# A Fourier filter and maxout MLP on one core: how batch 0 loads x, splits the weights and thresholds its spectrum

## The chip, the cores and the metric

The kernel runs on one core of a Trainium2 chip. The metric is the device time of one execution in microseconds (us). TensorE (PE in the profile), VectorE (DVE), ScalarE (ACT) and GpSimd (POOL) each run their own instruction queue in order; SyncE (SP) and ScalarE issue the DMAs.

## The reference, cut to what matters

```
X  = rfft(x, axis=1)                         # x: 8 batches, 3072 x 256, f32
Yr = X.real @ w_r - X.imag @ w_i + b_r
Yi = X.real @ w_i + X.imag @ w_r + b_i
Y  = sign(Y) * max(|Y| - 0.01, 0)            # on Yr and Yi apart: the soft threshold
y  = irfft(Y)                                # 24576 tokens x 256
h  = max(y @ w1, y @ w2, y @ w3)             # w1..w3: 256 x 768, float64
out = h @ w_out                              # w_out: 768 x 256, float64
```

The four MLP weights are given in float64.

## The kernel before, in words

The transform of 3072 points is split as 48 x 64. For each batch there are five stages. **Stage a** (`load_x`, `stage_a`) loads x in eight quarters q, transforms over the 48 and stores the result in DRAM (`a_d`). **Stage b** (`load_a`, `first_b` for batch 0) loads pairs of rows of it, k = 0 to 11, and transforms over the 64. **Stage w** (`first_w`, `soft_threshold`, `finish_w`) multiplies by w_r and w_i, adds the bias, thresholds at 0.01 and takes a maximum. **Stage q** (`first_q`) transforms back over the 64 and stores `z_d`. Then comes, chunk by chunk, the last transform (`load_z`, `split_z`, `inverse`) and the MLP (`up`, `down`).

Batches 1 to 7 go through this in f16 pairs (high and low halves), three products each, interleaved with the MLP of the batch ahead. Batch 0 has nothing to hide behind. It runs in f32 at the very start, and its code stands in `with in_order()`, where each engine's queue follows the order of the code; after that block the scheduler orders the queues.

The same start also prepares the weights. The float64 words of w1, w2, w3 and w_out come as pairs of 32-bit words; class `Weights` turns each of 18 units (12 of `w_up`, 6 of `w_dn`) into a scaled f16 pair. Its pieces are DVE work with a little ACT work: `exponent`, `combine`, `words`, for eight units `differ` (w1 - w3, w2 - w3), and `low`. Four units (w3) are instead transposed on TensorE in `turn`, which adds the two words' products up there. Each piece has a cost in a list, and `fill(budget)` in step k of batch 0 takes pieces off the list until the budget is spent; `fill` thus decides how much weight work a step carries. In step k the order on the queues is: stage b of k+1, the filling, stage w of k, stage q of k-1. So TensorE's product for stage q of k-1 (tile `pz`, line 580) needs the thresholded tile `uf` of k-1, and stands behind the products of stage w of k (tile `py`, lines 568 and 569).

At the start, the loads of batch 0's x go out on SP (r = 0) and ACT (r = 1), in rows of 2 KB, 96 of them a load; the f32 results leave in tiles `aq` and `zq`. `warm(36)` then runs 36 dummy products on a tile of zeros, and `load_fft_weights` loads w_r and w_i (`wst`), the bias, of which one row (partition 64) is written twice, and `qf`; after it `load_first_blocks(0)` loads the first table of stage b (`mb_all`). In `soft_threshold` DVE clips u to plus and minus 0.01 (`t`, line 633) and subtracts (line 634).

The lines of the weight work: 317 (`xe`), 320 (`xg`, ACT), 324 and 327 (`combine`), 334 and 335 (`words`), 341 (`differ`, two instructions), 347 (`turn`, TensorE), 351 and 357 (high halves, ACT), 354 (`turned`), 360 and 361 (`low`).

## Time and profile before

| | |
|---|---|
| median of 3 runs | 1837.19 us (1836.24 to 1837.34) |
| the profiled execution | 1839.4 us, span of its core 1837.6 us |
| TensorE busy in the span | 1788.9 us (97%) |
| VectorE busy | 1306.5 us (71%) |
| ScalarE busy | 961.7 us (52%) |
| granted TensorE clock, mean | 0.99 |

The profile is of one execution; times in it are microseconds from the span's start. Busy time of TensorE counts products that stream, so it tells where the engine stood still, not how well it was used. A row of the timeline has the start, the duration, the engine, the line, the operation and the tiles, and in brackets the idle time ahead of it with what ended that; for a queue of DMA issues (SPq, ACTq) the duration is that of issuing, not of the transfer.

### The profile page before, as it was taken

The numbers are of one execution on the slowest core, as the hardware profiler recorded it, in microseconds if no ns is written. First come the engines' busy times: TensorE is split into PE (matmuls) and PEld (weight loads), VectorE is DVE, ScalarE is ACT, GpSimd is POOL, SyncE is SP. The second block draws the span as 40 slices with busy tenths as digits, with TensorE's granted clock in tenths as the row PEclk, the third lists the DMA queues.
The fourth block names the chain that finished last, engine by engine and source line by source line (L and its number), as shares of the span: only waits on it lengthen the run. The fifth ranks groups of instructions, "written<-read, shape, count | busy, mean of one in ns | idle before, by whom it ended". The sixth has DMA issues, their size and how long they took to land.

```text
span 1837.6 us, 36331 instructions
## 1 busy us (share of the span) xinstructions
PE 1788.9 (97%) x14583; PEld 1287.7 (70%) x14583; DVE 1306.5 (71%) x2589; ACT 961.7 (52%) x1923; POOL 72.4 (4%) x120
## 2 busy tenths in 40 slices
PE   6988999999999999999999999999999999999999
PEld 2854777777677777767777776777767777777776
DVE  1898789667786688757886688866878568864443
ACT  1344666455555555455564565645655456544443
POOL 0001000000000000100001000000000000000000
PEclk8988999999999999999999999999999999999999
DMA  8734432233223323232322432223322312212110
GB/s 241 259 98 104 130 101 84 73 107 104 82 66 102 95 84 90 68 110 86 87 81 68 123 87 87 76 77 105 96 87 67 96 54 62 61 38 58 36 35 27
DMA packets 116443, 164.99 MB, mean 90 GB/s; under 512 B 13009, under 2 KB 88786, under 8 KB 116178
## 3 DMA queue, kind: packets, MB, share of 16 engines
q1 hardware_dynamic: 53122, 86.37, 17.1%
q10 hardware_dynamic: 63152, 76.31, 13.7%
q8 instruction: 114, 1.87, 0.4%
q14 instruction: 55, 0.45, 0.1%
HBM read 87.13 MB, written 75.50 MB: 88 GB/s over the span
## 4 chain that ended last, share of the span: by engine, by line
PE 72%; DVE 7%; issue 2%; DMA 1%; ACT 1%; ACTq 1%; SPq 0%; POOL 0%; DVEq 0%; POOLq 0%
PE pu L133 11%; PE pu L135 11%; PE pu L134 11%; PE pd L135 8%; PE pd L133 7%; PE pd L134 7%; PE py L134 2%; PE py L133 2%; PE py L135 2%; PE pa L485 2%; DMA xq<-in_x_dram 1%; DVE u L676 1%; PE pi L135 1%; DVE hh L128 1%; PE pi L133 1%
## 5 line engine op out<-in xcount | busy, mean ns | idle before, releaser
L133 PE MATMUL pu<-yh,w_all 128*128 128x384 f16 x1536 | 501.5, 327 | 5.3 <-DVE h L819 4.0
L134 PE MATMUL pu<-yl,w_all 128*128 128x384 f16 x1536 | 500.9, 326 | 2.4 <-DVE yl L128 2.1
L135 PE MATMUL pu<-yh,w_all 128*128 128x384 f16 x1536 | 500.3, 326 | 0.0
L127 ACT ACTIVATE hh<-h 128x384 f16<-128x384 f32 x384 | 200.4, 522 | 361.1 <-DVE h L819 354.1
L819 DVE TENSOR_TENSOR h<-pu,c 128x384 f32<-128x384 f32 x384 | 212.3, 553 | 174.9 <-PE pu L135 114.0
L135 PE MATMUL pd<-w_all,hh 128*128 128x256 f16 x1152 | 314.0, 273 | 8.4 <-DVE hh L128 8.2
L134 PE MATMUL pd<-w_all,hh 128*128 128x256 f16 x1152 | 314.2, 273 | 0.2 <-DVE w_all L361 0.2
L133 PE MATMUL pd<-w_all,hh 128*128 128x256 f16 x1152 | 313.9, 273 | 0.0
L128 DVE SCALAR_TENSOR_TENSOR hh<-h,hh 128x384 f16<-128x384 f32 x384 | 213.1, 555 | 105.5 <-ACT hh L127 104.2
L817 ACT ACTIVATE c<-pu 128x384 f32<-128x384 f32 x384 | 186.9, 487 | 132.3 <-PE pu L135 121.7
L133 PEld LDWEIGHTS <-w_all 128*128 128x128 f16 x1548 | 151.5, 98 | 113.5 <-issue 33.3
L135 PEld LDWEIGHTS <-w_all 128*128 128x128 f16 x1548 | 151.4, 98 | 104.6 <-issue 4.8
L134 PEld LDWEIGHTS <-w_all 128*128 128x128 f16 x1548 | 151.6, 98 | 87.4 <-issue 7.7
L676 DVE SCALAR_TENSOR_TENSOR u<-py,s1x,cs 64x256 f32<-64x256 f32 x308 | 148.7, 483 | 45.7 <-ACT cs L687 32.0
L133 PE MATMUL py<-wc_all,tt 128*128 128x256 f16 x504 | 137.4, 273 | 0.0
L134 PE MATMUL py<-wc_all,tt 128*128 128x256 f16 x504 | 137.4, 273 | 0.0
L135 PE MATMUL py<-wc_all,tt 128*128 128x256 f16 x504 | 137.4, 273 | 0.0
L133 PEld LDWEIGHTS <-hh 128*128 128x128 f16 x1152 | 112.8, 98 | 32.5 <-issue 2.4
L134 PEld LDWEIGHTS <-hh 128*128 128x128 f16 x1152 | 112.8, 98 | 30.9 <-issue 0.8
L135 PEld LDWEIGHTS <-hh 128*128 128x128 f16 x1152 | 112.8, 98 | 27.9 <-DVE hh L128 14.2
L846 ACT ACTIVATE o<-pd,s1u 128x256 f32<-128x256 f32 x192 | 83.5, 468 | 70.9 <-PE pu L135 26.1
L472 DVE TENSOR_REDUCE mxx<-xq 112x1 f32<-112x512 f32 x112 | 74.5, 678 | 46.6 <-DMA xq<-in_x_dram 42.2
(196 smaller groups left out, 3058.8 us busy)
## 6 DMA issues: line engine op xcount, KB each, us to landing
z_d<-zs ACTq DMA_DIRECT2D x96, 256.0 KB, 2.2
zq<-z_d SPq DMA_DIRECT2D x128, 192.0 KB, 3.1
out_dram<-o ACTq DMA_DIRECT2D x192, 128.0 KB, 2.3
a_d<-aq ACTq DMA_DIRECT2D x118, 192.0 KB, 3.2
aj<-a_d SPq DMA_DIRECT2D x86, 256.0 KB, 3.1
xq<-in_x_dram SPq DMA_DIRECT2D x114, 192.0 KB, 3.6
rw<-in_moe_w_dram SPq DMA_DIRECT2D x12, 384.0 KB, 6.3
mb_all<-in_dft_ib_dram SPq DMA_DIRECT2D x4, 384.0 KB, 5.4
```

The costliest lines, as they stand in the source:

```text
L127: nc.scalar.activation(out=hi, in_=src, func=AF.Copy, scale=scale)
L128: nc.vector.scalar_tensor_tensor(out=lo, in0=src, scalar=scale, in1=h, op0=ALU.mult, op1=ALU.subtract)
L133: nc.tensor.matmul(o, lh, rh, start=start, stop=False, **kw)
L134: nc.tensor.matmul(o, lh, rl, start=False, stop=False, **kw)
L135: nc.tensor.matmul(o, ll, rh, start=False, stop=stop, **kw)
L472: nc.vector.tensor_reduce(out=batch(b, "x")[0:XR, 2 * q4 + i:2 * q4 + i + 1], in_=xp, axis=AX.X, op=ALU.max, apply_absolute_value=True,)
L485: nc.tensor.matmul(pa[r][64 * c:64 * c + 64], fr[rows], xs[c][rows], start=True, stop=True)
L676: nc.vector.scalar_tensor_tensor(out=u[64 * c:64 * c + 64, j], in0=pk[r], scalar=inv[r], in1=c1[r], op0=ALU.mult, op1=ALU.add,)
L817: nc.scalar.activation(out=c1, in_=pu[0], func=AF.Relu)
L819: nc.vector.tensor_tensor(out=h32, in0=pu[1], in1=c1, op=ALU.max)
L846: nc.scalar.activation(out=o, in_=pd[t], func=AF.Copy, scale=st[b, "su"][1])
```

## The change

It has five parts, all in batch 0 and in the weight work. (1) x of batch 0 is loaded in four groups g, in rows of 8 KB (four tiles' worth of a partition at once), all on SP; `first_a` does stage a for a group with the same 32 products and 16 copies and stores each group with two DMAs in place of four. The tile `aq` is twice as wide with 2 buffers in place of 3 plus `zq`. (2) The five bias loads write each row once, and `load_first_blocks(0)` goes ahead of the loads of w_r and w_i. (3) `words` makes one f32 of a 64-bit word's two halves, so that `differ`, `low` and `turn` handle one word in place of two. (4) The threshold of steps 0 to 10 is two Relu activations on ACT and one subtraction on DVE. (5) The budgets change: the maxima of `w_dn` move from steps 7 and 8 to 5 and 6, step 10 has 1.5, step 11 carries no filling, and the filling behind the last stage q has 3.0 in place of 4.0. The zeros of `warm` are taken from `wsh`, which is written later.

```diff
 def load_fft_weights():
+        load_first_blocks(0)
...
-        for j in range(2):
-            for c in range(2):
-                nc.sync.dma_start(
-                    out=bias[64 * c:64 * c + 64, j, :], in_=rows[c].broadcast_to([64, D])
-                )
-        nc.sync.dma_start(out=bias[64:65, 1, :], in_=rows[0])
+        for c, j, r0, r1 in ((0, 0, 0, 64), (0, 1, 0, 64), (1, 0, 64, 128), (1, 1, 65, 128), (0, 1, 64, 65)):
+            nc.sync.dma_start(out=bias[r0:r1, j, :], in_=rows[c].broadcast_to([r1 - r0, D]))
...
             def words():
-                nc.vector.tensor_tensor(out=hw, in0=hw, in1=g, op=ALU.bitwise_or)
                 nc.vector.scalar_tensor_tensor(
-                    out=r, in0=lw, scalar=2.0**-52, in1=g.bitcast(F32), op0=ALU.mult, op1=ALU.mult
+                    out=r, in0=lw, scalar=2.0**-32, in1=hw, op0=ALU.mult, op1=ALU.add
                 )
+                nc.vector.scalar_tensor_tensor(
+                    out=m, in0=r, scalar=2.0**20, in1=t["g"].bitcast(F32), op0=ALU.add, op1=ALU.mult
+                )
             def differ():
-                for v, bv in zip((m, r), (self.raw[base][:, :, 1], self.raw[base][:, :, 0])):
-                    nc.vector.tensor_tensor(out=v, in0=v, in1=bv.bitcast(F32), op=ALU.subtract)
+                nc.vector.tensor_tensor(
+                    out=m, in0=m, in1=self.raw[base][:, :, 1].bitcast(F32), op=ALU.subtract
+                )
...
             def low():
-                nc.vector.tensor_tensor(out=m, in0=m, in1=hi, op=ALU.subtract)
-                nc.vector.tensor_tensor(out=lo, in0=m, in1=r, op=ALU.add)
+                nc.vector.tensor_tensor(out=lo, in0=m, in1=hi, op=ALU.subtract)
...
+    def first_x(g):
+        xv = x[0].rearrange("(n1 r g w n) d -> g w r n1 (n d)", n1=N1, r=2, g=4, w=2)[g]
...
+            for r in range(2):
+                nc.sync.dma_start(
+                    out=xw[64 * r:64 * r + N1, 2048 * g:2048 * g + 2048].rearrange("p (w m) -> p w m", w=2),
+                    in_=xv[:, r].rearrange("w p m -> p w m"),
+                )
...
+    def first_a(g):
+        aq = quad_tile("aq")
...
+        for c in range(2):
+            (nc.scalar if c else nc.sync).dma_start(
+                out=av[c], in_=aq[64 * c:64 * c + N1].rearrange("p (r m) -> p r m", r=2)
+            )
...
     def soft_threshold(k, u):
         t = fft.tile([P, 2, D], F32, name="t", bufs=1)
+        if k < NJP - 1:
+            nc.scalar.activation(out=t, in_=u, func=AF.Relu, scale=-1.0, bias=nlam)
+            nc.scalar.activation(out=u, in_=u, func=AF.Relu, scale=1.0, bias=nlam)
+            nc.vector.tensor_tensor(out=u, in0=u, in1=t, op=ALU.subtract)
...
-            elif 4 <= k < NJP:
-                fill(2.8)
+            elif 4 <= k < NJP - 2:
+                fill(3.0)
+            elif k == NJP - 2:
+                fill(1.5)
```

In the queues this stands as follows. First SP, from the loads of w_r and w_i on (`wst`; `mb_all` is the first table of stage b). Before:

```order
L185 DMA wst<-in_w_i_dram 128x256
L189 DMA bias<-in_b_r_dram 64x256
L189 DMA bias<-in_b_i_dram 64x256
...
L192 DMA bias<-in_b_r_dram 1x256
L193 DMA qf<-in_dft_ib_dram 128x256
L854 DMA mb_all<-in_dft_ib_dram 128x768
L284 DMA rw<-in_moe_w_dram 128x768 x8
```

and in the change, from batch 0's x on:

```order
L468 DMA w_all<-in_x_dram 48x2048 x6
L477 DMA xq<-in_x_dram 48x1024 x4
L923 DMA id_sb<-in_ident_dram 128x128
L498 DMA a_d<-aq 96x1x1024 x4
L891 DMA mb_all<-in_dft_ib_dram 128x768
L188 DMA wst<-in_w_r_dram 128x256
L188 DMA wst<-in_w_i_dram 128x256
...
L191 DMA bias<-in_b_r_dram 64x256 x2
L191 DMA bias<-in_b_i_dram 64x256
L191 DMA bias<-in_b_i_dram 63x256
L191 DMA bias<-in_b_r_dram 1x256
L192 DMA qf<-in_dft_ib_dram 128x256
```

The table now stands ahead of the weights and of the bias; the one-row bias load writes a row that no other load writes.

Second DVE, in steps 0 and 1 of batch 0 (`uf` is the tile that is thresholded, `mwu` the maxima of the weights). Before:

```order
L572 TENSOR_TENSOR uf<-py,bias 128x512
L633 TENSOR_SCALAR t<-uf 128x512
L634 TENSOR_TENSOR uf<-uf,t 128x512
L712 TENSOR_REDUCE mxu<-uf 128x1
L288 TENSOR_REDUCE mwu<-rw 128x1 x5
```

and in the change, where the subtraction follows the addition at once:

```order
L603 TENSOR_TENSOR uf<-py,bias 128x512
L667 TENSOR_TENSOR uf<-uf,t 128x512
L749 TENSOR_REDUCE mxu<-uf 128x1
L287 TENSOR_REDUCE mwu<-rw 128x1 x5
L603 TENSOR_TENSOR uf<-py,bias 128x512
```

while ACT has, in one of those steps:

```order
L577 ACTIVATE tf<-px 128x4x128
L580 ACTIVATE tf<-px 128x4x64
L665 ACTIVATE t<-uf,nlam 128x512
L666 ACTIVATE uf<-uf,nlam 128x512
L768 ACTIVATE zs<-pz 128x512
L769 DMA z_d<-zs 128x2x256
```

The two activations stand between DVE's addition and DVE's subtraction, and nothing was moved into the gap on DVE.

From the f16 split of batch 1's first pair (`ah` on ACT, `al` on DVE) to the end, the queues of all engines are the same row for row.

## Rows read from the trace of the kernel before

**Rows 1.** Busy time by stage, in six stretches from the span's start: busy us of each engine (in brackets the instructions), then the granted TensorE clock as a share of full speed, the DMA engines' mean busy share, and GB/s.

```profile
0.00:39.64 39.64, 21.56 (x101) 7.08 (x101) 8.67 (x14) 6.48 (x10) 2.61 (x7) 0.89 0.86 222
39.64:47.53 7.89, 7.89 (x34) 7.28 (x35) 0.00 (x0) 1.74 (x4) 0.00 (x0) 0.68 1.00 370
47.53:116.63 69.10, 62.91 (x316) 51.19 (x319) 63.40 (x141) 24.18 (x48) 0.57 (x3) 0.97 0.60 189
116.63:175.40 58.77, 51.97 (x309) 26.27 (x309) 57.59 (x151) 30.48 (x63) 5.65 (x6) 0.86 0.41 106
175.40:198.95 23.55, 23.36 (x182) 14.27 (x179) 11.39 (x34) 12.07 (x24) 3.77 (x4) 1.00 0.57 164
198.95:1837.60 1638.65, 1621.20 (x13654) 1181.63 (x13651) 1165.42 (x2250) 886.78 (x1776) 59.77 (x100) 1.00 0.28 79
```

**Rows 2.** Timeline of TensorE at the start: start us, duration us, engine, line, operation, tiles, count, and in brackets the idle time ahead and its releaser.

```profile
20.21 7.93 PE L859 MATMUL pw<-zero 128*128 128x512 f16 x36 [0.32 <-ACT aq L488]
39.64 3.75 PE L541 MATMUL px<-mb_all,ga_all 128*128 128x128 f32 x16 [11.50 <-DMA mb_all<-in_dft_ib_dram]
...
47.37 1.05 PE L541 MATMUL px<-mb_all,ga_all 128*128 128x128 f32 x8
...
52.57 1.05 PE L541 MATMUL px<-mb_all,ga_all 128*128 128x128 f32 x8
```

**Rows 3.** Timeline of SP's queue of DMA issues: start us, duration us of the issue, queue, line, tiles.

```profile
30.42 0.47 SPq L189 DMA_DIRECT2D bias<-in_b_i_dram  x1
35.52 0.29 SPq L192 DMA_DIRECT2D bias<-in_b_r_dram  x1
...
36.25 0.42 SPq L854 DMA_DIRECT2D mb_all<-in_dft_ib_dram  x1
```

**Rows 4.** Timeline of ACT's queue of DMA issues: the last store of batch 0's stage a, and the first loads of stage b, which wait for all the stores.

```profile
24.54 0.36 ACTq L492 DMA_DIRECT2D a_d<-zq  x1
28.87 1.45 ACTq L517 DMA_DIRECT2D ga_all<-a_d  x3
```

**Rows 5.** The loads of stage b into tile `ga_all`, from 0 to 60 us: time from issue to landing, shortest, median and longest.

```profile
DMA to landing us min/median/max: 4.5/6.2/8.5
```

**Rows 6.** Busy time by stretch, with the columns of rows 1: while batch 0's x lands in rows of 2 KB (2 to 18), while stores in rows of 4 KB make up most (18 to 22), while MLP weights land in rows of 3 KB (40 to 50), and while two loads of batch 1's x, in the same rows of 2 KB, go beside other loads (66 to 70).

```profile
2.00:18.00 16.00, 12.10 (x56) 3.17 (x56) 2.76 (x4) 3.67 (x5) 0.00 (x0) 1.00 1.06 212
18.00:22.00 4.00, 3.32 (x21) 1.29 (x18) 1.96 (x3) 1.26 (x3) 1.89 (x2) 1.00 1.03 386
40.00:50.00 10.00, 10.00 (x49) 9.19 (x49) 2.33 (x4) 2.62 (x6) 0.00 (x0) 0.77 1.01 374
66.00:70.00 4.00, 4.00 (x22) 3.24 (x22) 3.48 (x10) 2.10 (x4) 0.00 (x0) 1.00 1.13 389
```

**Rows 7.** Timeline of DVE in batch 0: one threshold and the first maximum of the weights behind it, the addition of step 3, then a `differ` and a `low` with what follows each.

```profile
47.57 0.69 DVE L572 TENSOR_TENSOR uf<-py,bias 128x512 f32<-128x512 f32 x1 [8.67 <-PE py L569]
48.29 0.43 DVE L633 TENSOR_SCALAR t<-uf 128x512 f32<-128x512 f32 x1
48.75 0.69 DVE L634 TENSOR_TENSOR uf<-uf,t 128x512 f32<-128x512 f32 x1
49.48 0.69 DVE L712 TENSOR_REDUCE mxu<-uf 128x1 f32<-128x512 f32 x1
50.08 0.54 DVE L288 TENSOR_REDUCE mwu<-rw 128x1 f32<-128x384 f32 x1
...
62.32 0.69 DVE L572 TENSOR_TENSOR uf<-py,bias 128x512 f32<-128x512 f32 x1 [1.43 <-PE py L569]
...
78.38 1.02 DVE L341 TENSOR_TENSOR rw<-rw 128x384 f32<-128x384 f32 x2
79.32 0.35 DVE L317 TENSOR_SCALAR xe<-rw 128x384 uint32<-128x384 uint32 x1
...
86.40 0.55 DVE L360 TENSOR_TENSOR rw<-rw,w_all 128x384 f32<-128x384 f32 x1
86.99 0.56 DVE L361 TENSOR_TENSOR w_all<-rw 128x384 f16<-128x384 f32 x1
87.46 0.68 DVE L572 TENSOR_TENSOR uf<-py,bias 128x512 f32<-128x512 f32 x1
```

**Rows 8.** Timeline of ACT: two activations back to back on tiles of 512 and 256 columns in PSUM, and one on 512 columns in SBUF that also reads a one-column tile.

```profile
64.45 0.60 ACT L546 ACTIVATE tf<-px 128x512 f32<-128x512 f32 x1 [0.44 <-PE px L541]
64.94 0.38 ACT L549 ACTIVATE tf<-px 128x256 f32<-128x256 f32 x1
...
198.21 0.71 ACT L127 ACTIVATE ah<-aj,s0x 128x512 f16<-128x512 f32 x1
```

**Rows 9.** Waits of TensorE from 47.53 to 116.63 us: for whom, us in total, times, longest.

```profile
PE pz L583 <- DVE uf L634: 5.3, 1, 5.3
PE pz L580 <- DVE uf L634: 0.8, 1, 0.8
```

**Rows 10.** Groups of DVE instructions by line and shape from 47 to 199 us (busy us in all, mean ns of one): `low`'s first instruction for w_out.

```profile
L360 DVE TENSOR_TENSOR rd<-rd,w_all 128x256 f32<-128x256 f32 x6 | 2.5, 411 | 0.0
```

**Rows 11.** TensorE alone in stretches of 2 us: busy us and instructions, granted clock, DMA share, GB/s.

```profile
30.00:32.00 2.00, 0.00 (x0) 0.75 0.53 175
...
160.00:162.00 2.00, 1.13 (x11) 1.00 0.00 0
162.00:164.00 2.00, 0.99 (x22) 1.00 0.97 220
164.00:166.00 2.00, 2.00 (x7) 0.53 1.03 253
```

More of the change, by code (lines that the diff above doesn't have):

```diff
@@ L345, in turn @@
                 for j in range(width // P):
-                    for v, first in ((m, True), (r, False)):
-                        nc.tensor.matmul(
-                            pt[:, j * P:j * P + P], v[:, j * P:j * P + P], id_sb, start=first, stop=not first
-                        )
+                    nc.tensor.matmul(
+                        pt[:, j * P:j * P + P], m[:, j * P:j * P + P], id_sb, start=True, stop=True
+                    )
                 t["p"] = pv = pt[:, 0:width].rearrange("p (f d) -> p f d", d=P)
@@ L466, in load_x @@
         st["x", q] = [xq[0:XR, c] for c in range(2)]
+    def first_x(g):
+        xv = x[0].rearrange("(n1 r g w n) d -> g w r n1 (n d)", n1=N1, r=2, g=4, w=2)[g]
+        xw = w_all.bitcast(F32)
+        if g < 3:
+            st["x0", g] = [xw[:, 2048 * g + 512 * i:2048 * g + 512 * i + 512] for i in range(4)]
+            for r in range(2):
[3 more added lines that the diff above has]
+                )
+            return
+        st["x0", g] = []
+        for w in range(2):
+            xq = fft.tile([P, 2, 2 * D], F32, name="xq", bufs=2)
+            for r in range(2):
+                nc.sync.dma_start(out=xq[64 * r:64 * r + N1].rearrange("p c m -> p (c m)"), in_=xv[w, r])
+            st["x0", g] += [xq[:, 0], xq[:, 1]]
@@ new lines, in first_a @@
+    def first_a(g):
+        aq = quad_tile("aq")
+        for i in range(2):
+            pa = [ff_tile("pa") for _ in range(2)]
+            for c in range(2):
+                for r in range(2):
+                    rows = slice(64 * r, 64 * r + N1)
+                    nc.tensor.matmul(
+                        pa[r][64 * c:64 * c + 64], fr[rows], st["x0", g][2 * c + i][rows], start=True, stop=True
+                    )
+            for r in range(2):
+                o = aq[:, 1024 * r + 512 * i:1024 * r + 512 * i + 512]
+                if r == 0:
+                    nc.scalar.activation(out=o, in_=pa[r][0:XR], func=AF.Copy)
+                else:
+                    nc.vector.tensor_copy(out=o, in_=pa[r][0:XR])
+        av = batch(0, "a").rearrange("k (r g c n) d -> g c k r (n d)", r=2, g=4, c=2)[g]
+        for c in range(2):
+            (nc.scalar if c else nc.sync).dma_start(
+                out=av[c], in_=aq[64 * c:64 * c + N1].rearrange("p (r m) -> p r m", r=2)
+            )
@@ L478, in stage_a @@
         b, q4 = divmod(q, NCH)
-        aq = quad_tile("zq") if q < NCH and q % 4 == 3 else quad_tile("aq")
+        aq = quad_tile("aq")[:, 0:NQ * D]
         xs = st["x", q]
@@ L486, in stage_a @@
         for r in range(2):
[L487 to L490 removed]
+            nc.scalar.activation(out=aq[:, r * 512:r * 512 + 512], in_=pa[r][0:XR], func=AF.Copy)
         for c in range(2):
[L492 removed]
+            nc.scalar.dma_start(
                 out=batch(b, "a")[:, 8 * q4 + 4 * c:8 * q4 + 4 * c + 4, :],
@@ L879, in fourier_maxout_kernel @@
         nc.sync.dma_start(out=fr, in_=fa)
+        nc.gpsimd.memset(nlam, -LAM)
         nc.gpsimd.memset(zero, 0.0)
-        for q in range(NCH):
-            load_x(q)
+        for g in range(4):
+            first_x(g)
         nc.sync.dma_start(out=id_sb, in_=ident)
-        for q in range(NCH):
-            stage_a(q)
+        for g in range(4):
+            first_a(g)
         warm(36)
@@ L952, in fourier_maxout_kernel @@
         warm(12)
-        fill(4.0)
+        fill(3.0)
         split_z(0, 2)
```

45 lines of the change are left out of this document (19 added, 26 removed).

## The prediction

> **What bounds the kernel now.** Read first the busy time by stage [rows 1]. After 198.95 us TensorE is busy 1621.20 of 1638.65 us at full clock, and from there the change leaves every queue as it was; I take that stretch as unchanged. All that can move lies in the first 198.95 us, in three places.
>
> Until 39.64 us TensorE waits for data: 21.56 us busy, of which 7.93 are the dummy products of `warm` [rows 1, 2]. What ended that wait is in the timelines. Stage b's first product starts at 39.64 us, released by the table `mb_all` [rows 2]. That table was issued at 36.25 us, because SP stood from 30.42 to 35.52 us at the one-row bias load, which has to wait for the load that wrote the same row [rows 3]. The other input was there sooner: ACT issued the loads of `ga_all` at 28.87 us, and the quickest took 4.5 us, so about 33.4 us [rows 4, 5]. Behind that stands batch 0's x: its 3072 x 256 f32 are 3.15 MB, and they moved at 212 GB/s with the DMA engines full (1.06), where other transfers reach 374 to 389 GB/s [rows 6].
>
> From 47.53 us, the end of the first `py`, to 116.63 us, where the maximum over all of batch 0 is taken, a step of TensorE is 5.20 us (47.37 to 52.57) [rows 2], but DVE is busy 63.40 of 69.10 us [rows 1]. Its last waits for TensorE are 8.67 us ahead of step 0 and 1.43 us ahead of step 3 [rows 7]; from then on DVE sets the pace, and TensorE loses 5.3 + 0.8 us to it at the end [rows 9].
>
> From 116.63 to 175.40 us DVE is busy 57.59 of 58.77 us, TensorE 51.97 with its clock at 0.86 [rows 1]: DVE-bound again. Then TensorE is full until 198.95 us.
>
> **The change part by part.**
>
> *Start.* Removing the double write takes SP's wait away, and `mb_all` now stands ahead of the weights and biases, so the table no longer sets the start; `ga_all` does. That alone moves stage b from 39.64 to 33.4 us: -6.3. What is late next is the chain x, stage a, stores, `ga_all`. How fast rows of 8 KB land when they are the only traffic, no row shows. Bounds: 212 GB/s as now, and 389 GB/s [rows 6]. I take 340: nearer to the upper end, since batch 1's x in rows of 2 KB is part of the 389, so neither its spacing nor its 48 partitions cap it alone. 3.15 MB take 14.9 us at 212 and 9.3 at 340: -5.6 (0 to -6.8). One queue instead of two costs nothing I can see: the 374 GB/s are mostly one queue's (SP). The ring of `aq` still holds the same amount of unsaved results (two double tiles for four single ones), so the store of one group still delays the copy of the next but one, as before. Stage b then starts near 27.8 us. Its first products run cold, as now: the clock had fallen by 30 to 32 us [rows 11], some 3 us after `warm` ended at 28.14 [rows 2], and the new chain leaves a gap of about that size too. If the gap closes, up to 2.4 us more are won: the first 16 products take 3.75 us for twice 0.89 warm. **Start: -11.9 us, from -6.3 to -15.**
>
> *Threshold.* On DVE one step now takes 0.72 (addition) + 0.46 (clip) + 0.73 (subtraction) + 0.60 (maximum) = 2.51 us, from 47.57 to 50.08 [rows 7]. In the change the clip goes, but the subtraction stands right behind the addition in DVE's queue and must wait for two activations. A 512-column activation from SBUF with a one-column operand takes 0.71 us, and the second starts some 0.11 us before the first ends [rows 8]: 0.60 + 0.71 = 1.31. With 0.1 for the two handovers (an estimate from the 0.03 between dependent DVE instructions there, 48.26 to 48.29) the step takes 0.72 + 1.41 + 0.73 + 0.60 = 3.46: +0.95 us. What is queued behind the waiting subtraction is the weight work, and TensorE's `pz` waits for the subtraction. Bounds: +0.6 (activations at the 0.60 of a PSUM source) and +1.7 (another activation of 0.7 ahead in ACT's queue). Steps 0 to 2 have the 1.43 us of slack ahead of step 3: 2.85 - 1.43 = +1.4. Steps 3 to 10 have none: 8 x 0.95 = +7.6. Both are on the path.
>
> *Weight work in batch 0's steps.* Up to the last step the queue does the same units as before. `differ` drops one of two instructions: two take 0.94 (78.38 to 79.32), so -0.47. `low` drops one of two: 1.06 for both (86.40 to 87.46), 0.47 for one, so -0.59 [rows 7]. Four units each: -4.2. `words` keeps two instructions, but the second now reads the first's result; a dependent instruction starts 0.03 after its forerunner ends and an independent one 0.08 before (48.29 against 50.08 [rows 7]), so +0.1 for six units, +0.6. The sum of this and the threshold is 1.4 + 7.6 - 4.2 + 0.6 = **+5.4 us for 47.53 to 116.63** (bounds 0 and +11). The new budgets move work within the steps; step 11 has none, but steps 4 to 10 carry what it had, so that is neutral while DVE is full. The two transposes lose half their products; TensorE has slack there: nothing.
>
> *Weight work behind it.* Four more `differ` (-1.9), four `low` (-1.9, at 0.47, since the interleaved order hides the handover) and six `low` of w_out at 0.41 less 0.08 of overlap (-2.0) [rows 7, 10]: -5.8. The smaller filling ahead of the first chunk leaves 1.0 us more for later. **-4.8 us**, bounds 0 (TensorE or batch 1's x sets the end) and -8 (the falls of the clock in this stretch vanish too).
>
> **Sum:** -11.9 + 5.4 - 4.8 = -11.3. The profiled execution is 1839.4 us, so 1828.1 there; it lies 2.2 above the median of the runs, 1837.19, against which I state the time: **1825.9 us**.
>
> [...] Rows of the trace: x at 212 GB/s, 2 KB rows, 64 KB from one partition's row to the next [rows 6]. [...]
>
> **Rivals.**
>
> [...] Then the start gains 6.3 and the sum is -6.3 + 5.4 - 4.8 = -5.7: 1831.5 us. Chance 0.25.
>
> *B, the round trip to ACT is hidden.* If DVE's wait costs as much as the clip it replaces, 47.53 to 116.63 us gains 4.2 - 0.6 and the sum is -11.9 - 3.6 - 4.8 = -20: 1817 us. For: ACT is busy 24.18 of 69.10 us [rows 1], so it is free when asked. Against: DVE's order, with nothing between addition and subtraction. Chance 0.10.
>
> *C, slower: TensorE's clock falls in the steps.* With DVE at 6.5 to 8.5 us a step and TensorE needing 5.2, TensorE would stand 1 to 3 us in every step from 4 on. The clock did fall at about 164 us after a stretch in which TensorE was busy 1.13 and 0.99 of 2 us [rows 11]. At the lower of its two levels, 1.2 GHz in place of 2.4, a step is 10.4 us, and TensorE instead of DVE sets the pace: about 3 us more in each of 8 steps, +24, so -11.3 + 24 = +13: 1850 us. [...]
>
> **How the numbers follow.** My forecast has 0.60, A 0.25, B 0.10, C 0.05. The range takes A and B with their margins and leaves C and the far ends of the bounds out: 1816 to 1833. What a measurement of this kernel can tell from no change is 0.2%, 3.7 us, so faster means below 1833.5. The forecast is below it but for a few of its bounds, A (1831.5) in most cases, B always: faster 0.88, same 0.07, slower 0.05.
>
> **What would show it.** Right: stage b's first product at 26 to 30 us, released by `ga_all`, and no wait of SP among the bias loads; x above 300 GB/s; some 1.4 us of idle DVE time ahead of each subtraction in steps 0 to 10, ended by ACT; the maximum over batch 0 about 74 us after the first `py`'s end, against 69.10; the stretch behind it shorter by 4 to 5 us; the last 1638 us as long as before. Wrong: stage b first released by something else, idle ahead of the subtractions under 0.5 us, a granted clock under 0.9 between steps 4 and 11, or a last stretch that differs by over 2 us.

## The result: slower, and the profile after

The prediction was wrong. The change takes 1851.03 us (median of 4 runs, 1849.29 to 1853.98) where the kernel before takes 1836.72 beside it: ratio 1.0080, 95% interval 1.0063 to 1.0098, so 14.7 us slower; forecast was 11.3 us faster. The profiled execution took 1851.66 us, its span is 1849.9.

Busy time by stage in the change, cut at the same events as [rows 1] (columns as there; the fourth cut, 190.00, is a round number):

```profile
0.00:42.29 42.29, 26.96 (x101) 8.50 (x101) 6.80 (x11) 5.84 (x9) 2.59 (x8) 0.95 0.81 188
42.29:50.50 8.21, 8.21 (x34) 7.51 (x35) 1.69 (x4) 2.04 (x5) 0.00 (x0) 0.66 0.84 274
50.50:130.11 79.61, 64.33 (x304) 50.82 (x307) 55.89 (x122) 38.47 (x70) 0.64 (x3) 0.96 0.58 184
130.11:190.00 59.89, 48.15 (x297) 26.52 (x298) 52.07 (x137) 30.77 (x63) 5.66 (x6) 0.86 0.40 106
190.00:213.92 23.92, 23.92 (x182) 14.46 (x178) 11.38 (x37) 11.50 (x24) 3.77 (x4) 1.00 0.56 161
213.92:1849.90 1635.98, 1619.77 (x13654) 1181.55 (x13651) 1164.91 (x2249) 886.95 (x1776) 59.79 (x100) 1.00 0.28 79
```

Read the lengths against [rows 1]: start 42.29 against 39.64 (+2.65), first products 8.21 against 7.89 (+0.3), batch 0's steps 79.61 against 69.10 (+10.5), the stretch up to batch 1's first split 83.81 against 82.32 (+1.5), the rest 1635.98 against 1638.65 (-2.7): +12.3 us of span. VectorE's busy time in the steps fell by 7.5 us (63.40 to 55.89) while the steps grew: it is no longer the work of VectorE that fills them.

**The start.** TensorE's timeline, then SP's queue of issues, then ScalarE, in the change (columns as in [rows 2, 3]):

```profile
42.29 3.75 PE L572 MATMUL px<-mb_all,ga_all 128*128 128x128 f32 x16 [5.21 <-DMA ga_all<-a_d]
58.71 2.04 PE L572 MATMUL px<-mb_all,ga_all 128*128 128x128 f32 x8 [3.03 <-DMA mb_all<-in_dft_ib_dram]
```

```profile
5.89 7.08 SPq L477 DMA_DIRECT2D xq<-in_x_dram  x4
21.21 0.36 SPq L923 DMA_DIRECT2D id_sb<-in_ident_dram  x1
21.70 8.88 SPq L498 DMA_DIRECT2D a_d<-aq  x4
30.63 2.74 SPq L891 DMA_DIRECT2D mb_all<-in_dft_ib_dram  x1
...
40.07 2.45 SPq L191 DMA_DIRECT2D bias<-in_b_i_dram  x2
...
44.20 4.16 SPq L283 DMA_DIRECT2D rw<-in_moe_w_dram  x8
...
51.44 0.35 SPq L891 DMA_DIRECT2D mb_all<-in_dft_ib_dram  x1
```

```profile
12.73 0.67 ACTq L498 DMA_DIRECT2D a_d<-aq  x1
...
17.22 0.56 ACTq L498 DMA_DIRECT2D a_d<-aq  x1
26.89 1.08 ACT L493 ACTIVATE aq<-pa 112x512 f32<-112x512 f32 x2 [9.88 <-DMA a_d<-aq]
...
30.04 0.72 ACTq L498 DMA_DIRECT2D a_d<-aq  x1
38.42 1.56 ACTq L548 DMA_DIRECT2D ga_all<-a_d  x3
```

The releaser is the forecast one, `ga_all`, and SP's 5 us among the bias loads are gone. But SP issues nothing from 12.97 to 21.21 us, behind the tenth load of x (the six loads of the first three groups have rows of 8 KB, the four of the last group, into `xq`, rows of 4 KB). ScalarE stores its halves of the first two groups at 12.73 and 17.22 us; SP's halves, which were ready at the same times, go out from 21.70. The third group's copies need the first group's tile and stand 9.88 us for that store. So the last stores leave at 30.04 (24.54 in [rows 4]) and `ga_all` is issued at 38.42 in place of 28.87. Then step 2 of batch 0 waits 3.03 us for the second table, issued at 51.44 behind eight MLP loads.

DMA traffic in the change (columns as in [rows 6]):

```profile
2.00:18.00 16.00, 11.19 (x38) 2.76 (x42) 2.77 (x4) 2.40 (x5) 0.00 (x0) 1.00 1.00 183
...
22.00:26.00 4.00, 2.22 (x10) 0.37 (x4) 0.00 (x0) 0.00 (x0) 1.69 (x2) 1.00 0.76 163
26.00:30.00 4.00, 2.47 (x6) 0.86 (x6) 2.58 (x4) 2.16 (x4) 0.14 (x1) 0.68 0.42 85
```

x lands at 183 GB/s where it landed at 212 [rows 6], not at 340, with the DMA engines as full; then they are less busy (shares 0.76, 0.42).

**The steps.** VectorE, then ScalarE, in step 0 (columns as in [rows 7, 8]), and the waits of TensorE from 50.5 to 130.11 us (as in [rows 9]):

```profile
50.51 0.69 DVE L603 TENSOR_TENSOR uf<-py,bias 128x512 f32<-128x512 f32 x1 [2.80 <-PE py L600]
52.80 0.69 DVE L667 TENSOR_TENSOR uf<-uf,t 128x512 f32<-128x512 f32 x1 [1.60 <-ACT uf L666]
53.53 0.69 DVE L749 TENSOR_REDUCE mxu<-uf 128x1 f32<-128x512 f32 x1
54.13 2.38 DVE L287 TENSOR_REDUCE mwu<-rw 128x1 f32<-128x384 f32 x5
```

```profile
51.30 0.72 ACT L665 ACTIVATE t<-uf,nlam 128x512 f32<-128x512 f32 x1 [4.05 <-DVE uf L603]
52.05 0.72 ACT L666 ACTIVATE uf<-uf,nlam 128x512 f32<-128x512 f32 x1
```

```profile
PE pz L611 <- DVE uf L667: 7.0, 5, 2.3
PE pt L209 <- DVE col L202: 3.8, 1, 3.8
PE px L572 <- DMA mb_all<-in_dft_ib_dram: 3.0, 1, 3.0
```

From addition to weight work the threshold takes 54.13 - 50.51 = 3.62 us (2.51 in [rows 7], 3.46 forecast): the activations follow each other (0.75 us apart) and do not overlap. Over all steps (VectorE's groups by line, from 50 to 131 us; columns as in [rows 10], at the end the idle time ahead and its releaser):

```profile
L667 DVE TENSOR_TENSOR uf<-uf,t 128x512 f32<-128x512 f32 x11 | 7.6, 692 | 17.1 <-ACT uf L666 17.1
```

VectorE stands 17.1 us ahead of eleven subtractions, 1.55 each.

### The profile page after: what moved, and what is told of

Its sections match the earlier page's. It is cut to its first block, busy times and chain, and to the rows that moved or that the text cites. A ratio compares the mean times of both kernels' runs of the same rounds, so it can differ in the third digit from the quotient of the medians.

```text
span 1849.9 us, 36236 instructions
## 1 busy us (share of the span) xinstructions
PE 1791.3 (97%) x14559; PEld 1289.4 (70%) x14559; DVE 1292.8 (70%) x2556; ACT 975.6 (53%) x1945; POOL 72.5 (4%) x121
## 4 chain that ended last, share of the span: by engine, by line
PE 71%; DVE 7%; issue 2%; DMA 2%; ACT 1%; ACTq 1%; SPq 0%; DVEq 0%
PE pu L133 11%; PE pu L135 11%; PE pu L134 11%; PE pd L135 7%; PE pd L133 7%; PE pd L134 7%; PE py L133 2%; PE py L134 2%; PE py L135 2%; PE pa L519 2%; DMA xq<-in_x_dram 1%; DVE u L713 1%; PE pi L135 1%; DVE hh L128 1%; PE pi L133 1%
## 5 line engine op out<-in xcount | busy, mean ns | idle before, releaser
L135 PE MATMUL pd<-wsh,yl 128*128 128x256 f16 x384 | 104.7, 273 | 0.0
```

The source lines that it names most:

```text
L135: nc.tensor.matmul(o, ll, rh, start=False, stop=stop, **kw)
```

## The experiments

Each was timed with the kernel before on the same chip. Only ratios are compared; 0.1% is 1.84 us, and us in the text that follow from ratios are worked out so.

| run | differs from | by | median us | ratio to before (95%) |
|---|---|---|---|---|
| the change | before | all five parts | 1851.03 | 1.0080 (1.0063-1.0098) |
| e1 | the change | part 1 undone | 1837.21 | 1.0011 (1.0001-1.0020) |
| e2 | the change | part 4 undone | 1839.70 | 1.0022 (1.0013-1.0032) |
| e3 | before | part 2 alone | 1835.19 | 0.9997 (0.9987-1.0007) |
| e4 | before | part 3 alone | 1825.37 | 0.9941 (0.9928-0.9953) |
| e5 | the change | x on two queues | 1842.25 | 1.0046 (1.0033-1.0059) |
| e6 | the change | stores on ScalarE | 1851.84 | 1.0096 (1.0082-1.0110) |
| e7 | before | parts 2, 3, table early | 1819.85 | 0.9922 (0.9909-0.9936) |
| e8 | e7 | part 4, gap filled | 1826.45 | 0.9957 (0.9945-0.9970) |
| e9 | e7 | part 5 | 1826.04 | 0.9946 (0.9934-0.9959) |
| e10 | e1 | x on one queue | 1842.92 | 1.0042 (1.0029-1.0054) |
| e11 | e7 | x from dense rows | 1820.14 | 0.9917 (0.9904-0.9931) |
| e12 | e7 | part 4, steps 4 to 10, filled | 1821.07 | 0.9929 (0.9916-0.9941) |
| e13 | e5 | a third store tile | 1840.64 | 1.0028 (1.0017-1.0040) |
| e14 | e7 | x over 128 partitions | 1820.26 | 0.9916 (0.9903-0.9930) |
| e15 | e7 | maxima in steps 5, 6 | 1821.72 | 0.9916 (0.9901-0.9931) |
| e16 | e7 | less filling in the steps | 1827.24 | 0.9957 (0.9943-0.9971) |
| e17 | e7 | more filling in the hole | 1826.32 | 0.9956 (0.9942-0.9970) |
| e18 | e15 | more filling in the steps | 1822.94 | 0.9930 (0.9916-0.9944) |

### The parts by themselves (e1 to e4)

e1, in `in_order` and with `load_x`, `stage_a`, `quad_tile` of before:

```diff
-        for g in range(4):
-            first_x(g)
+        for q in range(NCH):
+            load_x(q)
```

> The changed kernel with part 1 undone: x of batch 0 again in rows of 2 KB on SP and ACT, stage a and its tiles as before; parts 2 to 5 stay. Theory 1 (the new x path is what lost the start: it lands at 160 to 180 GB/s in place of 212, and the stores of its first groups stand behind it in SP's queue): x lands as before, ga_all is issued near 29 us and stage b's first product comes at 33 to 36 us in place of 42.3, so the time falls by 6 to 9 us, to 1842 to 1845. Rival (the table or the other loads hold the start whichever way x comes): first product still at 40 us or later and the time within 3 us of the changed kernel's 1851. Either way the stretch from the first py's end to the maximum over batch 0 stays near 79 us.

```profile
31.94 3.75 PE L537 MATMUL px<-mb_all,ga_all 128*128 128x128 f32 x16 [5.06 <-DMA ga_all<-a_d]
```

Theory 1, and more of it: TensorE's first product of stage b comes 10.4 us earlier, and the time falls by 0.69%, 12.7 us. Part 1 is the largest loss. The steps did not stay near 79 us as expected: from the first addition to the maximum over batch 0 they take 82.8 us (40.04 to 122.83), so a part of what the start gained is lost again there.

e2:

```diff
-        if k < NJP - 1:
-            nc.scalar.activation(out=t, in_=u, func=AF.Relu, scale=-1.0, bias=nlam)
...
-            return
```

> The changed kernel with part 4 undone: the threshold of all steps again as clip and subtraction on DVE. Theory 1 (the round trip to ACT is what lost the steps: 17.1 us of DVE idle ahead of 11 subtractions against 4.7 us of clips): DVE needs about 54.6 + 4.7 = 59 us there, TensorE its 63, and the stretch from the first py's end to the maximum over batch 0 falls from 79.6 to 66 to 71 us, so the time falls by 8 to 13 us, to 1838 to 1843. Rival (the loss there is the wait of step 2 for its table and the new budgets): the stretch stays above 75 us and the time falls by less than 5 us.

It gives back 0.58%, 10.7 us, as theory 1 has it for the time. The steps, 73.9 us from the first addition (49.2) to batch 0's scale (123.1) against 80.1 in the change, fall less than expected: the waits of TensorE there show what is left.

```profile
PE px L572 <- DMA mb_all<-in_dft_ib_dram: 4.2, 1, 4.2
PE pz L611 <- DVE uf L665: 2.2, 2, 1.2
```

`pz` waits 2.2 us in place of 7.0, but the table still costs 4.2.

e3 is before with the diff of `load_fft_weights`, e4 before with that of `combine`, `words`, `differ`, `turn` and `low`.

> The kernel before with part 2 alone: bias rows written once, first table ahead of the loads of w_r and w_i. Theory (SP's wait held the table back, and the loads of a_d are the next to be late): stage b's first product at 33 to 35 us in place of 39.6, and the time 4.5 to 6.5 us below the kernel before, near 1831. Rival (the loads of w_r, w_i, the bias and the MLP weights, now issued 5 us earlier, slow the last stores and the loads of a_d): first product at 37 us or later and less than 3 us won.

> The kernel before with part 3 alone (joined words); the costs in the list of pieces are left as before, so each step carries the same pieces. Theory (DVE is the bound in both stretches): the stretch from the first py's end to the maximum over batch 0 falls from 69.1 by 3 to 4.5 us, the one behind it (to the first split of batch 1) from 82.3 by 4 to 6, and the time by 7 to 10 us, to 1827 to 1830. Rival (behind the maximum, batch 1's x, the transposes' round trips and the clock set the end): the second stretch falls by less than 2 us, and the time by 2 to 5 us.

e3's first product comes at 32.1 us, even earlier than expected, yet the runs are no faster (-0.6 us, from -2.4 to +1.3). TensorE's waits from 28 to 112 us show one thing that takes it back:

```profile
PE px L538 <- DMA ga_all<-a_d: 4.5, 1, 4.5
PE px L538 <- DMA mb_all<-in_dft_ib_dram: 3.8, 1, 3.8
```

The second table, behind the same eight MLP loads, is now the late one. e4 wins 0.59%, 10.8 us: in all, joining the words is worth what the theory said. In its profile both stretches are shorter (by 3.1 us from the first addition to batch 0's scale, by 2.7 behind), the second by less than expected. They are 5.8 of the 14.5 us by which its profiled execution is shorter; 2.3 lie at the start, which e4 leaves as it was, and 6.4 in the last stretch (1632.20 us, 1638.65 in [rows 1]), which it was not meant to touch.

### One queue or long rows (e5, e6, e10, e13)

e5, and likewise for `xq`; e10 is the same question the other way round, in e1:

```diff
-                nc.sync.dma_start(
+                (nc.scalar if r else nc.sync).dma_start(
                     out=xw[64 * r:64 * r + N1, 2048 * g:2048 * g + 2048].rearrange("p (w m) -> p w m", w=2),
```

```diff
-                (nc.sync if b or r == 0 else nc.scalar).dma_start(out=xq[64 * r:64 * r + N1], in_=xv[r])
+                nc.sync.dma_start(out=xq[64 * r:64 * r + N1], in_=xv[r])
```

> The changed kernel with one edit: of batch 0's x, still in rows of 8 KB, the loads with r = 1 are issued by ACT, as before the change. Theory 1 (one queue for x is what lost the start: it fills, SP stands from 12.97 to 21.21 us with the stores behind it): with five loads a queue SP is free for the stores, x lands at 200 GB/s or more, stage b's first product comes at 32 to 37 us in place of 42.3, and the time falls by 5 to 11 us. Rival (the long rows themselves land slower, 160 to 180 GB/s, from whichever queue): x ends near 22 us again, the first product comes at 39 us or later and the time falls by less than 4 us.

> The kernel e1 (the change with x as before) with one edit: batch 0's x, still in rows of 2 KB, all on SP's queue. With e1 (2 KB, two queues), e5 (8 KB, two queues) and the change (8 KB, one queue) it makes the square of row length and queues. Theory 1 (the queue decides, not the row): x lands at 160 to 185 GB/s between 6 and 14 us as in the change, stage b's first product comes at 36 us or later in place of 31.9, and the time is 3 to 10 us above e1. Rival (the row decides): 200 GB/s or more there, the first product within 2 us of e1's, and the time within 2 us of e1.

DMA traffic from 6 to 14 us, in the change (8 KB, one queue), e5 (8 KB, two), e10 (2 KB, one) and e1 (2 KB, two):

```profile
6.00:14.00 8.00, 7.47 (x26) 1.87 (x29) 1.38 (x2) 1.19 (x2) 0.00 (x0) 1.00 0.99 169
```

```profile
6.00:14.00 8.00, 5.59 (x28) 1.57 (x32) 1.38 (x2) 1.19 (x2) 0.00 (x0) 1.00 1.00 215
```

```profile
6.00:14.00 8.00, 8.00 (x41) 2.50 (x34) 2.77 (x4) 2.39 (x4) 0.00 (x0) 1.00 1.01 250
```

```profile
6.00:14.00 8.00, 7.85 (x40) 1.58 (x33) 2.77 (x4) 2.48 (x3) 0.00 (x0) 1.00 1.07 215
```

The rate does not tell the story: one queue with 2 KB rows is not slower (250, some stores among it), only 8 KB rows on one queue are. e5 came out as its theory 1 has it: its first product at 34.93 us, its time 6.2 us below the change. The times make a plain square: one queue costs 0.34% with long rows (the change against e5) and 0.31% with short ones (e10 against e1), long rows with their grouping 0.38% and 0.35%; each some 6 us, with an interval of 3 to 4 us either way. What one queue holds up when x lands as fast stands in e10's SP queue and ScalarE:

```profile
15.54 0.46 SPq L888 DMA_DIRECT2D id_sb<-in_ident_dram  x1
16.12 1.43 SPq L488 DMA_DIRECT2D a_d<-aq  x3
```

```profile
19.98 0.60 ACT L484 ACTIVATE aq<-pa 112x512 f32<-112x512 f32 x1 [7.13 <-DMA a_d<-aq]
```

The stores stand behind all of x in SP's queue (from 13.87 us in the kernel before, from 16.12 here), and the copies stand 7.13 us for them (at most 1.73 in e1): the wait of the change, in 2 KB rows. Of the theory the time came true, the rate did not, nor did the first product at 36 us or later: it comes at 34.36 us (31.94 in e1). One execution says little there, for in the eight kernels that start as e7 does (e7 to e9, e12, e15 to e18) it comes anywhere from 30.91 to 34.34 us. That the wait for the stores is what the 5.7 us went to is argued from these rows, not shown. "DMA: Bandwidth & Descriptors" of the Trainium skill (Issuing engines are not separate DMA queues) says that spreading loads over issuing engines brings no bandwidth and saves only issue time. With 2 KB rows the trace agrees (215 with two, 250 with one); with 8 KB rows it does not (215 against 169).

e6 keeps x on SP and takes the stores away from there:

```diff
-            (nc.scalar if c else nc.sync).dma_start(
+            nc.scalar.dma_start(
```

> The changed kernel with one edit: all eight stores of batch 0's stage a are issued by ACT, so none stands behind x in SP's queue; x stays in rows of 8 KB on SP. Theory 1 (the start was lost by the stores that stand behind x, since the copies of the third group wait for the store of the first, 9.88 us): those waits fall below 3 us, the last stores are issued by 26 us in place of 30, ga_all by 33 in place of 38.4, stage b's first product comes at 36 to 38.5 us in place of 42.3 and the time falls by 4 to 6 us. Rival (x itself, which ends near 22 to 24 us, sets the start): the first product at 40 us or later, under 3 us won.

Both missed. TensorE's, SP's and ScalarE's rows:

```profile
48.12 3.75 PE L572 MATMUL px<-mb_all,ga_all 128*128 128x128 f32 x16 [10.44 <-DMA ga_all<-a_d]
```

```profile
30.79 6.31 SPq L283 DMA_DIRECT2D rw<-in_moe_w_dram  x8
```

```profile
22.28 6.08 ACTq L498 DMA_DIRECT2D a_d<-aq  x2
...
34.85 1.26 ACTq L498 DMA_DIRECT2D a_d<-aq  x2
```

The third group's copies wait 2.86 us for the first store in place of 9.88, as theory 1 has it. But now ScalarE's own queue stands: two stores take 6.08 us to issue, and the last two leave at 34.85 us (30.04 in the change). SP, free of stores, issues the MLP loads at 30.79 us in place of 44.20, among the last stores; the first product comes 5.8 us later than in the change, and the time is the same within the intervals: the later loads are earlier too, and no product waits for the second table any more. So the first product's time alone does not price the start, and taking the stores out from behind x was not by itself a cure.

e13 gives e5 one more store tile:

```diff
-        aq = quad_tile("aq")
+        aq = wc_all.bitcast(F32)[0:XR] if g == 2 else quad_tile("aq")
```

> The kernel e5 (x in rows of 8 KB on two queues) with one edit: the third group's results of stage a go to a third double tile (in the place of wc_all, which is not needed yet), so its copies need not wait for the store of the first group (2.80 us in e5). In the square of rows and queues the long rows cost some 6 us on two queues too, though x lands there at 215 GB/s as in rows of 2 KB. Theory 1 (what the grouping costs is the coarse ring of two double tiles): the waits of ACT for a_d<-aq fall below 1 us, stage b's first product comes at 32 to 33.5 us in place of 34.9, and the time falls by 2 to 5 us. Rival (it is the coarse transfers themselves: a group can start only when 8 KB rows of all its parts are there, and its stores of 384 KB take longer): first product within 1 us of 34.9, and the time within 2 us of e5's 1842.

The first product comes at 34.09 us (34.93 in e5); the ratio falls by 0.18%, but the intervals overlap, and ScalarE's waits for `a_d<-aq` fall to 2.28 us, not below 1 (2.80 and 2.22 in e5). Whether the rest of the price of long rows is their ring or their size stays open.

### What holds x at some 210 GB/s (e11, e14)

The loads of e11, then those of e14:

```diff
+        if b == 0:
+            xv = x[b].rearrange("(q r c n1 n) d -> q r n1 c (n d)", n1=N1, c=2, r=2, n=2)[q4]
```

```diff
+            xf = x[0].rearrange("(p q n) d -> q p (n d)", q=8, n=3)[q]
+            for r in range(2):
+                (nc.scalar if r else nc.sync).dma_start(out=xw[64 * r:64 * r + 64], in_=xf[64 * r:64 * r + 64])
```

> The kernel e7 with batch 0's x read from other addresses: rows of 2 KB as before, as many bytes, on the same two queues, but the 48 rows of a load lie one behind the other (2 KB apart) in place of 64 KB apart; what batch 0 computes is then of other elements. Theory 1 (the distance of 64 KB between rows is what holds x at 200 to 215 GB/s): x lands at 300 GB/s or more, its last product comes 4 us or more earlier, stage b starts at 28 to 31 us in place of 34.3, and the time falls by 2 to 5 us. Rival (48 of 128 partitions, or the first reads, or two queues hold it): 190 to 225 GB/s as before and the time within 2 us of e7.

> The kernel e7 with batch 0's x loaded in another shape: the same 3.15 MB in 16 loads on the same two queues, but over 64 partitions each, so 128 in all in place of 96, in rows of 3 KB; what batch 0 computes is then of other elements. In e11 the distance of the rows changed nothing. Theory 1 (the partitions that the loads reach hold x at 190 to 215 GB/s; the MLP weights, on 128 partitions in rows of 3 KB, reach 374): x lands at 280 GB/s or more from 6 to 14 us and its last product comes 4 us earlier than in e7 (20.8 us). Rival (nothing but x is read then, and whatever is read first lands at this rate, or two queues hold it): 190 to 240 GB/s and the last product at 19 us or later.

From 6 to 14 us, e11 and then e14:

```profile
6.00:14.00 8.00, 7.34 (x36) 1.58 (x32) 2.30 (x4) 2.48 (x3) 0.00 (x0) 1.00 1.07 217
```

```profile
6.00:14.00 8.00, 6.52 (x35) 1.54 (x32) 2.23 (x4) 2.48 (x3) 0.00 (x0) 1.00 1.04 244
```

Neither reaches 280, and neither time differs from e7. The measure is loose: the same stretch has 188 GB/s in e7 and up to 229 in other kernels with the loads of the kernel before. e11 lies within that, e14 a little above it. So the 64 KB between rows do not hold x, and the 96 partitions account for a small part at most; what does stays open. "DMA: Bandwidth & Descriptors" of the Trainium skill (Latency and other measured facts) gives copies between tensors in HBM whose rows lie 512 KiB apart 207 GB/s, and 214, which it calls full, with a padded distance, so there the loss is small too; it has no figure for 64 KB, and here that distance cost nothing that shows.

### Part 2 with the table, and the threshold with its gap filled (e7, e8, e12)

e7 is before with parts 2 and 3 and

```diff
+        load_first_blocks(1)
         for n in range(8):
             w_up.load(n)
...
-                load_first_blocks(1)
```

> The kernel before with parts 2 and 3, and the second table of stage b (mb_all, for steps 3 to 5 of the tables) issued ahead of the eight loads of MLP weights instead of behind them. Parts 2 and 3 apart gave -0.3 and -10.1 us against the kernel before. Theory 1 (the 7.5 us that part 2 wins at the first product are lost because step 2 then waits 3.8 us for the second table): with the table ahead, that wait is gone, stage b starts at 32 us and 4 to 7 us more than in part 3 alone are kept: 15 to 17 us below the kernel before, 1818.5 to 1821. Rival (the DMA engines are full from 38 to 75 us, so whatever is moved ahead makes another load late: w_r and w_i, ga_all or the MLP weights): another wait of 3 us or more takes its place and the time stays within 3 us of part 3 alone, 1823 to 1827.

0.9922, 14.3 us below before: faster than both kernels. It lies 3.5 us below e4, short of the expected gain over part 3 alone. No product waits for a table; TensorE's waits for `ga_all` are 6.4 us in two.

e8 moves the subtraction of `soft_threshold` to the head of `finish_w`, and the maxima or the filling of a step between the two; e12 does the same in steps 4 to 10 alone:

```diff
             turn_units()
+            if k < NJP:
+                stage_w(k)
...
             if k < NJP:
-                stage_w(k)
                 finish_w(k)
```

> The kernel e7 (parts 2 and 3, second table early) with the two activations of part 4, but DVE's weight work of the step is placed between the addition and the subtraction in place of ahead of the addition. Theory 1 (the activations lost time only since DVE had nothing to do meanwhile): the idle time ahead of each subtraction falls from 1.5 to under 0.3 us from step 1 on, DVE saves the clips (0.46 each, some 3 to 4 us in the steps where it is full), and the time is 1 to 4 us below e7. Rival (what the products of the next steps need comes later, since the subtraction now waits for the weight work too, and TensorE stands at pz): TensorE's waits for uf grow to over 8 us, and the time is 2 to 8 us above e7.

> The kernel e7 with the threshold's two activations on ACT in steps 4 to 10 alone, where DVE is full, and the filling of those steps between addition and subtraction; maxima and columns stay ahead of the addition, and steps 0 to 3 and 11 are as in e7. In e8, where all steps were so, TensorE waited 7.3 us for columns, and the last step's filling stood ahead of its maximum. Theory 1 (those two were e8's loss, and the clips saved, 0.46 x 7, count where DVE is full): 1 to 4 us below e7. Rival (the addition of the next step now waits for TensorE instead, 15.1 us in e8, since filling no longer runs ahead while TensorE works): 1 to 6 us above e7.

VectorE's groups in e8 (40 to 116 us):

```profile
L569 DVE TENSOR_TENSOR uf<-py,bias 128x512 f32<-128x512 f32 x12 | 8.3, 690 | 15.1 <-PE py L566 15.1
...
L710 DVE TENSOR_TENSOR uf<-uf,t 128x512 f32<-128x512 f32 x11 | 7.5, 685 | 2.0 <-ACT uf L632 2.0
```

The idle time ahead of the subtraction is gone (2.0 in place of 17.1), but it stands ahead of the addition now, and e8 is 6 us above e7: the rival's size, though not its `pz` (1.6 us; TensorE waits 7.3 us for columns). In e12 the additions wait 9.2 us (4.5 in e7), and its time is e7's. Moved to ScalarE, the threshold won nothing in any form tried.

### Part 5 (e9, e15 to e18)

e9 is e7 with part 5. That part also lowers the cost that the list gives `differ` and `low` (0.93 to 0.47), so a budget buys more pieces. e15 moves only the maxima, e16 sets only the budgets of the steps, with the costs of before; e17 and e18 go the other way (`fill(4.0)` to 6.0 behind the last stage q; `fill(2.8)` to 3.6 in e15's steps).

```diff
-            elif 4 <= k < NJP:
-                fill(2.8)
+            elif 4 <= k < NJP - 2:
+                fill(3.0)
+            elif k == NJP - 2:
+                fill(1.5)
```

> The kernel e7 (parts 2 and 3, second table early) with part 5: the new costs and budgets, w_dn's maxima in steps 5 and 6, no filling in step 11. Theory 1 (part 5 is a cost of its own: the prices of the other parts, measured one by one, add to +12 us of the change's +14.7): DVE carries more in steps 4 to 10, TensorE waits at pz in several of them, and the time is 1 to 4 us above e7. Rival (it is a gain, hidden so far by the other parts: the 4.5 us for which TensorE stands at the last pz go): the time is 1 to 4 us below e7, near 1817.

> The kernel e7 with one half of part 5: the maxima of w_dn in steps 5 and 6 in place of 7 and 8, with the filling of 1.8 there. All of part 5 cost 4 to 6 us in e9. Theory 1 (the earlier maxima cost nothing: the same work, two steps earlier): within 2 us of e7. Rival (w_dn's first units can be made earlier only if their loads have landed, and DVE is in arrears by then, so TensorE waits at pz and pt): 2 to 5 us above e7.

> The kernel e7 with the other half of part 5: budgets of 3.0 in steps 4 to 9 (1.8 in 7 and 8 stays), 1.5 in step 10 and none in step 11; costs as in e7. Theory 1 (less filling in all by step 11 moves weight work behind the maximum over batch 0, where DVE is the bound as well, and the gain of an emptier last step is given back): within 2 us of e7. Rival (this is the half that costs): 3 to 6 us above e7, with the stretch from that maximum to the first split of batch 1 longer by as much.

Part 5 costs 0.24%, 4.4 us, on top of e7; the maxima cost nothing; taking filling out of the steps as e16 does costs 0.35%, 6.4 us. The steps and the stretch behind them, in e7, in e9 and then in e16:

```profile
41.90:109.60 67.70, 61.60 (x304) 49.85 (x306) 60.78 (x137) 23.85 (x48) 0.57 (x3) 0.98 0.65 216
109.60:187.80 78.20, 70.30 (x483) 40.84 (x476) 63.38 (x170) 42.55 (x87) 9.43 (x10) 0.93 0.48 132
```

```profile
39.70:109.30 69.60, 62.75 (x308) 50.30 (x310) 61.15 (x136) 23.62 (x48) 0.55 (x3) 0.98 0.66 213
109.30:189.70 80.40, 69.80 (x476) 40.33 (x469) 62.87 (x169) 42.31 (x86) 9.44 (x10) 0.92 0.46 127
```

```profile
38.94:103.60 64.66, 60.95 (x308) 49.11 (x310) 57.67 (x128) 22.32 (x45) 0.67 (x3) 1.00 0.71 230
103.60:190.00 86.40, 73.45 (x480) 40.10 (x472) 67.31 (x179) 45.05 (x90) 9.42 (x10) 0.94 0.42 119
```

In e16 some 3 us of VectorE's work leave the steps (60.78 to 57.67). The steps win 3.0 us by it and the stretch behind loses 8.2, though VectorE is not full there (67.31 of 86.40). Part of that is seen where TensorE's products wait for single weight tiles, here ScalarE's high halves:

```profile
PE pu L133 <- ACT w_all L354: 3.4, 2, 1.9
```

This is not what part 5 does in e9, where VectorE's work hardly changes sides (60.78 to 61.15 and 63.38 to 62.87) and yet the steps grow by 1.9 us and the stretch behind by 2.2. Which of the new costs, the budgets and the smaller filling in the hole that is, no run separates.

> The kernel e7 with one number: the filling behind the last stage q, where TensorE waits for z to go to DRAM and back, is 6.0 in place of 4.0 (part 5 makes it 3.0). In e7 DVE is busy 8.30 of the first 10 us there and TensorE's first pi waits 3.4 us for zh. Theory 1 (DVE has idle time in that hole, so work put there is free and less is left for the stretch behind): 1 to 3 us below e7. Rival (the filling delays the split of z, which the first chunk waits for, by as much as it saves): within 2 us of e7, or up to 3 us above.

> The kernel e15 (e7 with w_dn's maxima in steps 5 and 6, which cost nothing) with the filling of 2.8 in steps 4, 7 to 11 raised to 3.6. Where e16 took some 3 us of filling out of the steps, the steps won 3.8 us and the stretch behind lost 8.2. Theory 1 (work ahead of the maximum costs less than work behind it): the steps lose 3 to 5 us, the stretch behind wins more, and the time is 1 to 4 us below e15's 1821.7. Rival (DVE is the bound in both, so it is an even exchange, or TensorE's clock falls in the longer waits): within 1.5 us of e15 or up to 5 us above.

The exchange does not turn round: e17 is 6.2 us above e7, beyond its rival, and e18 within the interval of e15. In e18 the steps take 5.5 us more of VectorE's work and are 4.1 us longer than in e15, and the stretch behind is 3.7 shorter: an even exchange, where e16's was a bad one. Why 2.0 of budget in the hole cost that much was not settled.

## Why the prediction was wrong, step by step

**The start, forecast -11.9, is the step that failed.** Its first half was right in the trace and empty in time: part 2 brings the first product to 32.1 us (forecast 33.4, -6.3), but alone wins 0.6 us, in part since step 2 then waits 3.8 us for the second table. "What is late next" was asked for the first product, not for the next load in SP's queue. Its second half had the sign wrong: forecast -5.6, measured +12.7 (e1). The sentence that failed is "One queue instead of two costs nothing I can see". It looked at bytes a second. The square of e1, e5, e10 and the change shows about half of the loss with the one queue, half with the long rows. What the rows show on one queue is that SP issues none of the stores until x is out, and that these hold the ring of store tiles, so "as before" was wrong for the ring too; but e6, with the stores taken away from SP, won nothing, so how much of the price that wait is stays open. The other failed sentence is the 340 GB/s, a value between two rows that were no rows of this transfer: some 212 held for two queues, and 183 to 201 came on one (the change, e6, e2; from 2 to 18 us). Rival A (x lands at 212 as before, 1831.5 us) was nearer in the rate and still missed the time by 20 us, as it shared the error on the queue. A small slip beside it: 3.75 us less twice 0.89 is 2.0, not the 2.4 that the far bound of the start has for a closed gap.

**The threshold, forecast 1.4 + 7.6 = +9.0, measured +10.7 (e2).** Right in mechanism. In the traces of the change and e2 the steps differ by 6.2 us of it; where the rest lies was not found. The forecast round trip was too short by the overlap: 1.41 us for the round trip was taken from activations on two different tiles [rows 8]; here the second writes in place what the first reads, and starts 0.03 us after its end. That this is why is read from the code and was not tested. Rival B is refuted; e8 and e12 show that even a filled gap does not win.

**The joined words, forecast -4.2 + 0.6 - 5.8 = -9.4, measured -10.8 (e4).** Right in the total, and in the steps (3.1 us in the trace, forecast 3.6). Behind them the trace gives 2.7 us of the 5.8 forecast, and the rest came where the forecast had nothing, so the total is right in part by luck.

**The budgets, forecast neutral but for 1.0 us, measured +4.4 (e9).** Wrong: "neutral while DVE is full" took both stretches as bound by VectorE's sum of work. In e9 that sum stays where it was and both stretches grow; why is open.

**The stretch behind the steps, forecast -4.8, measured +1.5.** The step that failed is "DVE-bound again". VectorE's work there did fall, from 68.98 to 63.45 us (57.59 + 11.39 in [rows 1], 52.07 + 11.38 above), and the stretch did not. TensorE's waits in it, from 130.6 to 213.9 us, are 5.5 us for the split of z (`zh`), 2.9 for `h` and 1.9 for the scale of w_r and w_i (`ec`); in the kernel before, from 117.1 to 198.95 us, the longest are 2.5 for `zl` and 1.9 for `h`. With part 4 undone (e2) the wait for `zh` is the same (5.3), and in e9 it is 4.5 where e7 has 3.4. In all its waits there are 11.6 us (6.7 before). So TensorE waits on the chain from the maximum through z to the last transform and the MLP, which the forecast did not count; what lengthened that chain stays open.

The five prices add to 12.7 - 0.6 - 10.8 + 10.7 + 4.4 = +16.4 us against +14.7 measured; each has an interval of 2 to 4 us either way, so the closeness says little. Rival C, the clock, did not happen: the granted clock is 0.96 over the steps (0.83 in the lowest stretch of 10 us, 90 to 100); that its 1850 us lie beside the measured 1851.03 is luck. The last stretch differs by 2.7 us with the same queues, a little more than the 2 us that I allowed. It varies from one kernel's profile to the next (1638.65 us before, 1636.90 in e3, 1635.98 in the change, 1632.50 in e1); why is open.

## What to carry to other kernels

Price a queue by what stands behind its loads, not by its bytes a second alone: before joining transfers on one issuing engine, list the stores that follow there and the ring of tiles that waits for them. When a wait at the start goes, look for the next load in the same queue before the gain is booked; and when work is moved behind a barrier, ask who waits for single pieces of it there, not only whether the engine has time. An element-wise operation given to another engine in the midst of a dependent chain costs two handovers, so look first for operations to remove, which is where this change's one gain came from.

## What the runs showed of the hardware

- SP issued ten loads of x (3.15 MB, in rows of 8 and 4 KB) by 12.97 us and its next, which needs none of their data, at 21.21. That a queue with so much under way holds up its engine's next issue is my reading; the profile names no cause but other DMAs that landed. With 2 KB rows, all on SP (e10), the sixteen loads themselves were issued over 14.3 us (1.19 to 15.49), and the next came right behind, at 15.54.
- From 6 to 14 us, rows of 8 KB landed at 169 GB/s (the change), 179 (e6) and 186 (e2) from one queue and at 215 (e5) and 232 (e13) from two; rows of 2 KB at 250 (e10, with some stores) from one and 188 to 229 from two over the runs with the same loads, and at 217 with rows 2 KB in place of 64 KB apart (e11). The MLP weights reach 374 later in the same kernel [rows 6].
- Two activations of 0.72 us, the second in place on what the first reads, start 0.75 us apart; two of 0.60 and 0.38 us on other tiles start 0.49 us apart [rows 8].
